# Loads of q and k into alternate partitions, and an evacuation that writes in token order

## The chip, the core and the metric

The kernel runs on one core of a Trainium2 chip. The metric is device time in microseconds (us). Before the change it is 179.21 us, the median of 3 runs (177.88 to 180.92).

The core's engines work in parallel, each through its own instructions in order. PE is the matmul engine (PEld its weight loads), DVE the vector engine, ACT the scalar engine, POOL the GpSimd engine; SP issues nearly all DMAs, through one queue. Matmuls read SBUF and write PSUM. DVE and ACT read PSUM and write SBUF. Copying a PSUM result into SBUF is called an evacuation here.

## The reference

Attention with a causal window of 128 keys and 4 sink keys, then an RWKV channel mix on its output:

```python
# q, k, v: [4, 8, 768, 64] float32; n_sink 4, window 128
scores = scale * np.matmul(q, k.transpose(0, 1, 3, 2))
keep = is_sink | in_window                    # is_sink: key < 4; in_window: 0 <= query - key < 128
a = softmax(np.where(keep, scores, -1e9))
x = np.matmul(a, v)                           # then laid out as [4, 768, 512]
xk = mu_k * x + (1.0 - mu_k) * x_prev         # x_prev: x one token earlier, zeros first
xr = mu_r * x + (1.0 - mu_r) * x_prev
k = np.maximum(xk @ w_k, 0.0)                 # w_k: 512 x 1024
v = k * k @ w_v                               # w_v: 1024 x 512
out = sigmoid(xr @ w_r) * v                   # w_r: 512 x 512
```

## The kernel before

The work is cut into 12 units: 4 batches of 3 tiles with 256 tokens each. A unit u goes through these stages, named by their lines.

- **Loads.** `load` brings q, k and v of a unit into float32 buffers, three of each kind. v comes in two DMAs over 128 partitions in pieces of 256 B (line 396). Of q and k the units that `by_dma` names (k from unit 4 on, q from unit 8 on) come the same way (line 406). The others, k of units 0 to 3 and q of units 0 to 7, come through line 418: two DMAs, w = 0 and 1, one for each half of the heads. A partition takes four tokens in succession, so that each piece is 1 KB; 64 partitions hold the 256 tokens of one half of the heads. Unit 0 is loaded in twice as many DMAs of 128 KB, the others in DMAs of 256 KB. `load_weight` brings the weights in pieces of 2 KB (line 437), 1 MB in a DMA.
- **Prepare.** For each half of what a partition holds: a cast to bf16 (lines 603 and 606, on ACT, DVE or POOL), four PE transposes into one PSUM bank (line 631), and one evacuation into `kt` or `qt` (line 639, on ACT or DVE), which holds the two head pairs with head dimension on partitions and tokens in order along the row. Units that `by_dma` names use a DMA transpose (line 620) in place of the last two. For the first tile of a batch POOL copies the sink keys out of `kt` (line 670).
- **Attend.** Scores on PE (line 716), exponentials on ACT (`e`, line 768), the mask on DVE (line 782), values on PE (line 801), then a reciprocal and a scaling on DVE (lines 815 and 818).
- **Mix and channel mix.** PE transposes `x` (line 841), ACT or DVE evacuates it into `xt` (line 850), DVE makes `xk` and `xr` (lines 868 and 879), PE multiplies by w_k (line 930), ACT takes the relu (line 940), DVE squares it (line 952), PE multiplies by w_r (line 961) and w_v (line 979), DVE combines and SP stores (lines 988 and 995).

The order on every engine is written out by hand: `ORDER` lists operation numbers for PE, DVE, ACT, POOL and SP, and `CHOICE` says which engine does an operation that could run on several. `Plan.schedule` follows these lists and only decides which buffer is used and where filler matmuls go (line 999; they keep PE busy at the start and compute nothing). On SP a DMA that has to wait holds all later ones. What decides when the q and k of a unit can be used is therefore: the place of its two DMAs in SP's list, the queue in front of them, the cast, the transposes, and the evacuation of line 639. The scores of a unit need `kt` and `qt`, and PE's next instructions stand behind those scores.

There are 24 evacuations at line 639: 19 on ACT and 5 on DVE. 28 DMAs come from line 418.

Of the kernel before, what the change touches and what calls it, by code (L numbers as in the profile page):

```python
# [305 lines left out]
def kernel(  # L306
# [55 lines left out]
    buf = P.buf  # L362
# [5 lines left out]
    def dve(n, rate=1.04):  # L368
        return 64.0 + rate * n

    def act(n):
        return 67.0 + 0.833 * n
# [13 lines left out]
    def by_dma(name, u):  # L386
        return u in (KD if name == "k" else QD)

    def load(u, names, rank, h0=0, h1=H):
        b, T = divmod(u, NT)  # L390
        for name in names:
            key = (name, u)
            if name == "v":
                for g in range(2):
                    s0 = 256 * T + 128 * g
                    P.op("SP", 560.0, lambda key=key, g=g, s0=s0: nc.sync.dma_start(
                        out=buf[key][:, g, :, :],
                        in_=v[b, :, s0:s0 + 128, :].rearrange("h p d -> p h d")), rank,
                        service=1330.0, descs=1024, take=[] if g else [("vs", key)],
                        hold=[key] if g else [], writes=[(name, u, g)])  # L400
                continue
            src = {"k": k, "q": q}[name]
            if by_dma(name, u):
                for g in range(2):
                    s0 = 256 * T + 128 * g
                    P.op("SP", 560.0, lambda key=key, src=src, g=g, s0=s0: nc.sync.dma_start(
                        out=buf[key][:, 4 * g:4 * g + 4, :, :].rearrange("p h j d -> p (h j) d"),
                        in_=src[b, :, s0:s0 + 128, :].rearrange("h p d -> p h d")), rank,
                        service=1330.0, descs=1024, take=[] if g else [(name + "s", key)],
                        hold=[key] if g else [], writes=[(name, u, g)])  # L410
                continue

            rows = src[b, :, 256 * T:256 * T + 256, :].rearrange(
                "(w l) (p j) d -> w p l (j d)", w=2, j=4)
            c0, c1 = h0 // 4, h1 // 4
            for w in range(2):
                P.op("SP", 400.0 + 20.0 * (c1 - c0), lambda key=key, rows=rows, w=w: (
                    nc.sync.dma_start(  # L418
                        out=buf[key][64 * w:64 * w + 64, h0:h1].rearrange(
                            "p (l x) j d -> p l (x j d)", x=2),  # L420
                        in_=rows[w][:, 2 * c0:2 * c1])), rank,
                     service=128 * (c1 - c0) * 3.33 + 45.0, descs=128 * (c1 - c0),
                     take=[] if h0 or w else [(name + "s", key)],
                     hold=[key] if h0 or w else [],
                     writes=[(name, u, c, w) for c in range(c0, c1)])
# [14 lines left out]
    for i, what in enumerate(LOADS):  # L440
        if what[0] == "w":
            load_weight(what, i - 100)
        elif what == "kq0":
            load(0, "kq", -100, 0, 4)
            load(0, "kq", -99.5, 4, 8)
        else:
            load(int(what[-1]), what[:-1], i - 100)
# [7 lines left out]
    for i, src in enumerate((moe_mu_k, moe_mu_r)):  # L455
        P.op("ACT", 450.0, lambda i=i, src=src: nc.scalar.dma_start(
            out=rows8[NC * i:NC * i + NC, :], in_=src.rearrange("(c p) -> c p", p=128)), -100,
# [124 lines left out]
    for i in range(4):  # L582
        j = i % 2
# [5 lines left out]
    for i in range(4):  # L589
        j = i % 2  # L590
# [4 lines left out]
    def prepare(u, rank):  # L595
        b, T = divmod(u, NT)
        for name, half in (("k", 0), ("q", 0), ("k", 1), ("q", 1)):
            key, psk = (name + "t", u), ("prep", u, name, half)
            raw, rk = (name, u), (name + "b", u)
            hs = slice(4 * half, 4 * half + 4)  # L600
            def cast(copy, raw=raw, rk=rk, hs=hs, half=half, name=name):
                if by_dma(name, u):
                    return lambda: copy(
                        out=buf[rk][:, half, :, :].rearrange("p h d -> p (h d)"),
                        in_=buf[raw][:, hs, :, :].rearrange("p h j d -> p (h j d)"))
                return lambda: copy(
                    out=buf[rk][:, half, :, :].rearrange("p (j a) d -> p a j d", a=2),
                    in_=buf[raw][:, hs, :, :].rearrange("p (a x) j d -> p a (x j) d", a=2))

            P.op("ACT", act(512), cast(nc.scalar.copy), rank + half,  # L610
                 alts={"ACT": (act(512), cast(nc.scalar.copy), False),
                       "DVE": (dve(512, 0.52), cast(nc.vector.tensor_copy), True),
                       "POOL": (600.0, cast(nc.gpsimd.tensor_copy), True)},
                 take=[] if half else [(name + "b", rk)],
                 hold=[raw] + ([rk] if half else []),
                 reads=[(name, u, half)] if by_dma(name, u) else [(name, u, half, w) for w in range(2)],
                 writes=[rk + (half,)])

            if by_dma(name, u):
                P.op("SP", 1200.0, lambda key=key, rk=rk, half=half: nc.sync.dma_start_transpose(  # L620
                    out=buf[key][:, :, half, :],
                    in_=buf[rk][:, half, :, :].rearrange("p h d -> p (h d)")), rank + half,
                    service=930.0, descs=512, lag=1450.0, room=1200, reads=[rk + (half,)],
                    take=[] if half else [(name + "t", key)],
                    hold=[rk] + ([key] if half else []), writes=[key + (half,)])
                continue

            def transpose(half=half, psk=psk, rk=rk):
                ps = buf[psk].bitcast(BF16)[:, 0:512].rearrange("p (j t) -> p j t", j=4)
                for j in range(4):  # L630
                    nc.tensor.transpose(  # L631
                        out=ps[:, j, :], identity=ident,
                        in_=buf[rk][:, half, 2 * j:2 * j + 2, :].rearrange("p a d -> p (a d)"))

            P.op("PE", 225.0, transpose, rank + half, lag=PE_LAG, take=[("bank", psk)],
                 reads=["ident", rk + (half,)], writes=[psk], hold=[rk])

            def evacuate(copy, half=half, psk=psk, key=key):
                return lambda: copy(  # L639
                    out=buf[key][:, half::2, :, :].rearrange(  # L640
                        "p c g (t j) -> p c j (g t)", j=4),
                    in_=buf[psk].bitcast(BF16)[:, 0:512].rearrange(
                        "p (j c t) -> p c j t", c=2, j=4))

            P.op("ACT", 600.0, evacuate(nc.scalar.copy), rank + half,
                 alts={"ACT": (600.0, evacuate(nc.scalar.copy), False),
                       "DVE": (625.0, evacuate(nc.vector.tensor_copy), False)},
                 hold=[psk] + ([key] if half else []),
                 take=[] if half else [(name + "t", key)],
                 reads=[psk] + ([key + (0,)] if half else []), writes=[key + (half,)])  # L650
# [15 lines left out]
        def sink_keys():  # L666
# [10 lines left out]
            out=buf[psk].rearrange("p (h d) -> p h d", h=H), lhsT=spread,  # L677
# [3 lines left out]
            out=vsink[b % 2][:, :, 0:D], op=ALU.mult, in1=hmask[:, :, 0:D],  # L681
# [370 lines left out]
```

## Time and profile before

| | |
|---|---|
| median of 3 runs | 179.21 us |
| the profiled execution's own time | 178.31 us |
| span of that execution, first to last instruction | 176.6 us |
| PE busy | 161.1 us (91%) |
| DVE busy | 157.1 us (89%) |
| ACT busy | 134.6 us (76%) |
| POOL busy | 19.7 us (11%) |
| bytes by DMA | 33.83 MB, mean 192 GB/s |

The span leaves 1.7 us of the execution's time around it. "Busy" is the time in which an engine had at least one instruction under way. The DMA share of a stretch is the time that all packets took divided by the time of 16 DMA engines; it can go over 1 where packets of one engine overlap. Times of a row start at the beginning of the span.

### The profile page before, as it was taken

The page shows a single profiled execution, that of the slowest core. Times are in us where ns is not written, and L with a number is a line of the kernel's source. Part 1 is how long each engine was busy: PE and PEld are TensorE (multiplying, and loading weights), DVE is VectorE, ACT ScalarE, POOL GpSimd, SP SyncE. Part 2 cuts the span into 40 slices and gives each one's busy share as a digit, 9 for nine tenths or more (in the row PEclk, how much of TensorE's full clock was granted, in tenths as well). Part 3 has the DMA queues.
Part 4 walks back from the last instruction along what each step waited for, and adds up shares of the span by engine and source line. Part 5 has one row for each costly group of instructions (what it writes and reads, how often), then busy time and mean ns, then how long its engine had stood idle before and what let it go on. Part 6 is the DMA issues. An engine that isn't in the chain of part 4 may idle for free.

```text
span 176.6 us, 4238 instructions
## 1 busy us (share of the span) xinstructions
PE 161.1 (91%) x1603; PEld 102.9 (58%) x1603; DVE 157.1 (89%) x399; ACT 134.6 (76%) x200; POOL 19.7 (11%) x45
## 2 busy tenths in 40 slices
PE   7875668889979999999999999999999999999992
PEld 2334445655545756765655777575466576677551
DVE  5579998999979998999999999998999799997851
ACT  2383899999799999799889999666768949845020
POOL 7513001020212200333100000000000100000000
PEclk9998799999999999999999999999999999999999
DMA  3799999979999999989989789587888953130043
GB/s 91 208 236 236 387 224 315 317 248 240 213 229 198 231 166 231 241 173 186 205 197 261 138 170 272 111 197 185 210 203 205 226 116 114 39 142 0 2 178 119
DMA packets 75844, 33.83 MB, mean 192 GB/s; under 512 B 63912, under 2 KB 70320, under 8 KB 75824
## 3 DMA queue, kind: packets, MB, share of 16 engines
q1 hardware_dynamic: 75808, 33.56, 82.4%
q8 instruction: 12, 0.20, 0.5%
q14 instruction: 8, 0.07, 0.2%
q10 hardware_dynamic: 16, 0.00, 0.0%
HBM read 24.12 MB, written 6.29 MB: 172 GB/s over the span
## 4 chain that ended last, share of the span: by engine, by line
PE 55%; ACT 16%; DMA 8%; DVE 8%; SPq 6%; issue 3%; POOL 0%; DVEq 0%; ACTq 0%; POOLq 0%
PE bank L930 16%; PE bank L979 16%; PE bank L961 8%; SPq L418 6%; DMA qs<-in_q_dram 5%; ACT qt L639 5%; PE bank L801 5%; ACT e L768 5%; PE sc L716 4%; DMA ks<-in_k_dram 3%; DVE xr L879 2%; PE bank L841 2%; ACT kt L639 2%; PE bank L756 2%; ACT xt L850 1%
## 5 line engine op out<-in xcount | busy, mean ns | idle before, releaser
L930 PE MATMUL bank<-xk,wk_sb 128*128 128x256 bf16 x384 | 51.0, 273 | 2.6 <-ACT wk_sb L568 1.7
L768 ACT ACTIVATE e<-sc 128x1024 bf16<-128x1024 f32 (+1 forms) x48 | 45.5, 978 | 3.4 <-PE sc L716 3.4
L979 PE MATMUL bank<-wv_h,kk 128*128 128x512 bf16 x184 | 46.4, 379 | 0.1
L930 PEld LDWEIGHTS <-wk_sb 128*128 128x128 bf16 x384 | 35.5, 98 | 13.1 <-issue 2.3
L940 ACT ACTIVATE rl<-bank 128x512 bf16<-128x512 f32 x44 | 26.4, 619 | 8.3 <-PE bank L930 5.1
L782 DVE TENSOR_TENSOR e<-e,mask 128x1024 bf16<-128x1024 bf16 (+1 forms) x48 | 30.2, 641 | 0.4 <-ACT e L768 0.4
L979 PEld LDWEIGHTS <-kk 128*128 128x128 bf16 x184 | 16.8, 98 | 14.9 <-issue 0.6
L961 PE MATMUL bank<-wr_sb,xr 128*128 128x512 bf16 x96 | 24.2, 379 | 0.1
L879 DVE SCALAR_TENSOR_TENSOR xr<-td,mu_all,xt 128x256 bf16<-128x256 bf16 x48 | 22.9, 492 | 0.1
L967 ACT ACTIVATE th<-bank 128x512 f32<-128x512 f32 x24 | 14.5, 618 | 10.3 <-PE bank L961 10.3
L879 DVE SCALAR_TENSOR_TENSOR xk<-td,mu_all,xt 128x256 bf16<-128x256 bf16 x48 | 21.9, 487 | 0.1
L952 DVE TENSOR_TENSOR kk<-rl 128x512 bf16<-128x512 bf16 x48 | 19.9, 429 | 0.5 <-ACT rl L940 0.4
L818 DVE TENSOR_TENSOR x<-bank,rec 128x256 bf16<-128x256 f32 x48 | 19.4, 418 | 0.5
L639 ACT COPY qt<-bank 128x512 bf16<-128x512 bf16 x13 | 17.3, 1333 | 2.9 <-PE bank L631 2.9
L988 DVE SCALAR_TENSOR_TENSOR ob<-th,bank 128x512 f32<-128x512 f32 x23 | 15.7, 683 | 3.7 <-PE bank L979 2.9
L801 PE MATMUL bank<-vb,e 128*128 128x65 bf16 x352 | 16.2, 193 | 2.0 <-DVE e L782 2.0
L801 PEld LDWEIGHTS <-e 128*128 128x128 bf16 x352 | 13.8, 97 | 5.3 <-DVE e L782 2.3
L716 PE MATMUL sc<-qt,kt 64*128 64x128 bf16 (+1 forms) x256 | 14.5, 242 | 2.6 <-ACT qt L639 1.1
L716 PEld LDWEIGHTS <-kt 64*128 64x128 bf16 x256 | 9.8, 96 | 7.9 <-issue 4.4
L961 PEld LDWEIGHTS <-xr 128*128 128x128 bf16 x96 | 9.0, 98 | 8.7 <-issue 0.6
L850 ACT COPY xt<-bank 128x512 bf16<-128x512 bf16 x16 | 9.5, 594 | 2.3 <-PE bank L841 2.2
L868 DVE TENSOR_TENSOR td<-xt 128x512 bf16<-128x512 bf16 x24 | 10.2, 434 | 0.8 <-ACT xt L850 0.8
(71 smaller groups left out, 160.3 us busy)
## 6 DMA issues: line engine op xcount, KB each, us to landing
vs<-in_v_dram SPq DMA_DIRECT2D x24, 256.0 KB, 5.1
out_dram<-ob SPq DMA_DIRECT2D x23, 256.0 KB, 2.9
qs<-in_q_dram SPq DMA_DIRECT2D x22, 256.0 KB, 4.8
ks<-in_k_dram SPq DMA_DIRECT2D x22, 256.0 KB, 5.5
w<-in_moe_w_k_dram SPq DMA_DIRECT2D x2, 1024.0 KB, 12.2
w<-in_moe_w_v_dram SPq DMA_DIRECT2D x2, 1024.0 KB, 9.3
w<-in_moe_w_r_dram SPq DMA_DIRECT2D x1, 1024.0 KB
ks<-in_k_dram SPq DMA_DIRECT2D x4, 128.0 KB, 2.9
```

The source lines that it names most:

```text
L639: return lambda: copy(out=buf[key][:, half::2, :, :].rearrange("p c g (t j) -> p c j (g t)", j=4), in_=buf[psk].bitcast(BF16)[:, 0:512].re ...
L716: nc.tensor.matmul(out=sc[:, a, o0:o1], lhsT=lhs[rows], rhs=rhs[rows], start=u not in BIAS, stop=True, skip_group_check=u in BIAS)
L768: nc.scalar.activation(out=buf[ek][:, :, lo:], in_=buf[sck][:, :, lo:], func=AF.Exp, scale=scale)
L782: nc.vector.tensor_tensor(out=at, in0=at, in1=m, op=ALU.mult)
L801: nc.tensor.matmul(out=o[:, g, a, :], lhsT=e[:, a, e0:e0 + 128], rhs=rhs, start=(T == 0 and i == 0), stop=(i == len(blocks) - 1), skip_gro ...
L818: P.op("DVE", dve(256), lambda ok=ok, rk=rk, c=c: nc.vector.tensor_tensor(out=buf["x", u][:, :, 128 * c:128 * c + 128].rearrange("p g (a d ...
L879: nc.vector.scalar_tensor_tensor(out=buf[key][:, c0 + 2 * i, :], in0=buf[tk][:, i, :], scalar=mu[w][:, c0 + 2 * i:c0 + 2 * i + 1], in1=xt[ ...
L930: nc.tensor.matmul(out=ps[:, i, :], lhsT=wk_sb[:, c, 128 * f:128 * f + 128], rhs=xk[:, c, :], start=(c == 0), stop=(c == NC - 1), skip_gro ...
L940: nc.scalar.activation(out=buf[rk], in_=buf[psk].rearrange("p (i t) -> p i t", i=2), func=AF.Relu)
L952: P.op("DVE", dve(512, 0.52), lambda f2=f2, rk=rk: nc.vector.tensor_tensor(out=buf["kk", u][:, 2 * f2:2 * f2 + 2, :], in0=buf[rk], in1=buf ...
L961: nc.tensor.matmul(out=buf[psk], lhsT=buf["xr", u][:, c, 128 * g:128 * g + 128], rhs=wr_sb[:, c, :], start=(c == 0), stop=(c == NC - 1))
L979: nc.tensor.matmul(out=buf[psk], rhs=wv_h[:, f, :], lhsT=buf["kk", u][:, f, 128 * g:128 * g + 128], start=(f == 0), stop=(f == NF - 1))
```

## The change

The destination of the two loads of line 418 changes from partitions 0 to 63 (w = 0) and 64 to 127 (w = 1) to the even (w = 0) and the odd (w = 1) partitions. Source, size of the pieces and number of DMAs stay.

A transposed partition is a column of the PSUM bank, so the columns of the two halves of the heads now alternate. The evacuation's access patterns change with that. Before, it reads runs of 64 adjacent bf16 columns and writes each run at a step of four elements (8 bytes). After, it writes runs of 256 adjacent elements and reads, for each group of four, one element from each of the four transposes: a step of 128 elements (256 bytes) inside the group, and of two elements (4 bytes) from group to group.

```diff
@@ load, line 418
-                        out=buf[key][64 * w:64 * w + 64, h0:h1].rearrange(
+                        out=buf[key][w::2, h0:h1].rearrange(
                             "p (l x) j d -> p l (x j d)", x=2),
                         in_=rows[w][:, 2 * c0:2 * c1])), rank,
@@ prepare, line 639
             def evacuate(copy, half=half, psk=psk, key=key):
                 return lambda: copy(
                     out=buf[key][:, half::2, :, :].rearrange(
-                        "p c g (t j) -> p c j (g t)", j=4),
+                        "p c g (t j) -> p c (g t) j", j=4),
                     in_=buf[psk].bitcast(BF16)[:, 0:512].rearrange(
-                        "p (j c t) -> p c j t", c=2, j=4))
+                        "p (j t c) -> p c t j", c=2, j=4))
```

The instructions on every engine, their order, their number and what they wait for are the same in both kernels; only the access patterns of these two operations differ.

## Prediction

> **What bounds the kernel now.** I read the chain of waits first, then a table of engine times by stage, the groups by form, and ACT's order of time in the stage where it is full. The chain, pieces in order of time (start, length, what):
>
> ```profile
> 9.73 5.72 DMA ks<-in_k_dram
> ...
> 16.89 1.31 DVE kt L639
> 18.24 0.62 PE sc L716 x6
> ...
> 20.71 1.31 ACT kt L639
> ...
> 39.09 8.96 DMA qs<-in_q_dram
> ...
> 48.65 1.30 ACT qt L639
> ```
>
> Until 57 us the end is set by three things in turn: loads of q and k (5.72 and 8.96 us of waiting), evacuations of line 639, and ACT's other work. From 57 to 83 the chain alternates between ACT and DVE; from 83 on it holds only PE, so what is saved earlier is kept and nothing more is won there. The stages, with their busy times, granted clock, DMA share and rate:
>
> ```profile
> core 0: us, PE busy (x) PEld busy (x) DVE busy (x) ACT busy (x) POOL busy (x), PEclk, DMA share, GB/s
> 0.00:20.00 20.00, 15.04 (x120) 7.95 (x121) 14.71 (x43) 9.84 (x11) 7.59 (x27) 0.91 0.86 216
> 20.00:36.00 16.00, 11.43 (x148) 8.57 (x146) 14.82 (x36) 15.98 (x21) 0.61 (x1) 1.00 1.02 288
> 36.00:48.00 12.00, 11.32 (x108) 6.24 (x106) 11.71 (x29) 10.82 (x16) 1.75 (x2) 1.00 1.04 244
> 48.00:57.00 9.00, 7.74 (x72) 4.41 (x71) 7.76 (x16) 8.66 (x12) 2.12 (x4) 1.00 1.12 213
> 57.00:83.00 26.00, 25.59 (x270) 17.48 (x268) 25.12 (x64) 24.79 (x38) 6.07 (x7) 1.00 1.13 206
> ```
>
> ACT is full from 20 to 36 us (15.98 of 16). DVE stands right behind it: 14.82 there, and 11.71 of 12 in the next stage. So freeing ACT is worth only what DVE has idle, and what the loads allow.
>
> **The evacuations.** Groups by form (busy, mean ns of one):
>
> ```profile
> L639 ACT COPY qt<-bank 128x512 bf16<-128x512 bf16 x13 | 17.3, 1333 | 2.9 <-PE bank L631 2.9
> ...
> L815 DVE RECIPROCAL rec<-bank 128x4 f32<-128x4 f32 x48 | 7.8, 176 | 3.1 <-PE bank L801 2.5
> ...
> L850 ACT COPY xt<-bank 128x512 bf16<-128x512 bf16 x16 | 9.5, 594 | 2.3 <-PE bank L841 2.2
> ...
> L639 DVE COPY qt<-bank 128x512 bf16<-128x512 bf16 x3 | 3.9, 1294 | 0.5 <-PE bank L631 0.5
> ...
> L944 DVE TENSOR_SCALAR rl<-bank 128x512 bf16<-128x512 f32 x4 | 2.7, 686 | 0.4 <-PE bank L930 0.4
> ```
>
> Line 639 moves as many elements as line 850, which reads and writes without a step, yet takes 1333 ns against 594. Its read is already in runs of 64, so I put the 0.7 us down to the write at 8-byte steps; that ACT and DVE take nearly the same (1333, 1294), though their stepless rows differ, fits a cost that lies in the memory. The change removes that step and adds another, a read of PSUM at 256 bytes. No row shows such a read at size. Bounds: at best it costs nothing, 594 ns on ACT and 415 on DVE, as line 850 has there. The nearest row with any step is line 639 itself, 1.31 us: no change. The far end is line 815, which reads four values 260 bytes apart in 176 ns, while a copy of eight adjacent ones (line 557) takes 134: if the whole difference were the step, 10 ns an element, 5 us an evacuation; the reciprocal itself explains it better. Nothing excludes a loss. I take 0.65 us on ACT and, from line 944, 0.69 on DVE, since every row that writes in runs lies there and the far end rests on one row with another explanation.
>
> How much of ACT's time an evacuation holds is seen in its order of time:
>
> ```profile
> 20.71 1.31 ACT L639 COPY kt<-bank 128x512 bf16<-128x512 bf16 x1
> 21.73 1.13 ACT L568 ACTIVATE wk_sb<-w 128x1024 bf16<-128x1024 f32 x1
> ...
> 24.77 0.63 ACT L940 ACTIVATE rl<-bank 128x512 bf16<-128x512 f32 x1
> 25.24 0.43 ACT L700 ACTIVATE es<-bank 128x256 bf16<-128x256 f32 x1
> ```
>
> The next instruction starts 1.02 us after an evacuation, and 0.47 us after a stepless 512-element one. So each evacuation frees about 0.5 us of ACT and shortens the wait of whoever needs it by 0.65.
>
> [...]
>
> **The loads.** Rates by stretch:
>
> ```profile
> 4.00:6.00 2.00, 2.00 (x7) 0.54 (x6) 0.66 (x2) 0.00 (x0) 1.87 (x7) 1.00 0.65 212
> 12.00:14.00 2.00, 0.90 (x14) 0.54 (x14) 1.46 (x6) 1.51 (x2) 0.00 (x0) 1.00 1.13 229
> ...
> 18.00:20.00 2.00, 1.89 (x25) 1.45 (x25) 2.00 (x7) 1.61 (x3) 0.00 (x0) 0.63 1.05 386
> ```
>
> While loads of line 418 queue (12 to 14 us) they move 229 GB/s with all 16 DMA engines held, 1.13 x 16 / 229 = 79 ns for each KB; spaced by SP's issue (4 to 6 us) a KB takes 0.65 x 16 / 212 = 49 ns; weights, over 128 partitions, go at 386 GB/s. So queued loads into 64 adjacent partitions slow each other. The change spreads each over the whole height. Bounds: 229 (no change) and 386; below 229 I have no row, and nothing excludes it. I take the middle, 300: 256 KB take 0.87 us in place of 1.14, 0.27 less for each DMA. The piece size, the number and SP's issue time (0.6 us each) stay, so I cost the issue at nothing.
> [...]
>
> **The sum, stage by stage**, where the advance is the smallest that any needed engine allows:
> - 0 to 20: k of unit 1 lands after four queued DMAs, 4 x 0.27 = 1.1 us earlier, but DVE is full from 14 to 16, so its `kt` evacuation at 16.89 moves only by idle time (0.2) and by what the earlier evacuations give (0.4, held by v's arrival), and is 0.6 shorter: 1.2 us.
> - 20 to 36: ACT frees 5 x 0.5 = 2.5 us. DVE has 1.2 idle and 0.4 from its one evacuation, 1.6 in all. I take 1.1: 2.3 in all.
> - 36 to 48: PE waits at 45.25 for k of unit 3, and the load of q ends the 8.96 us wait. By then 8 + 3 queued DMAs have gained 11 x 0.27 = 3.0 us, more than 2.3, so the loads don't eat the advance. PE and DVE are full: 0.
> - 48 to 57: four evacuations on ACT and one on DVE; PE is idle 1.26, DVE 1.24. I take 1.0: 3.3.
> - 57 to 83: four on ACT (two on the chain, at 63.86 and 68.11), but DVE has 0.9 idle and PE 0.4: 0.5, so 3.8.
> - after 83: two on ACT, beside a full PE: 0.
>
> 178.31 - 3.8 = 174.5 us for an execution like the profiled one, which lies 0.90 under the median of the runs: 175.4 us as a median. The cast, transposes and sink copy read the same amounts and cost nothing more; the clock of 0.63 at 18 to 20 us may move by some tenths either way.
>
> **The rivals.** (2) The loads reach the weights' rate: 256 KB in 0.68 us, 0.46 less; 45.25 then never binds and the first stage gives a little more. DVE still limits: 4.6 in all, 174.6. (3) The loads stay at 229: then k of unit 3 lands at 44.5 as before and PE's 2.3 us are lost waiting for it; left are 0.7 (the shorter `qt` at 48.65), 1.0 and 0.5: 2.2, so 177.0. For it: each DMA still has only 64 rows. (4) The stepped read costs what the stepped write did: ACT stays full, loads alone give 0.9, 178.3. (5) Slower: the read costs more than the write did. ACT has no slack from 20 to 36 and 0.3 from 48 to 57, so every 0.1 us above 1.31 costs 0.1 for each of 5 + 4 + 2 evacuations; at 1.65 us it is 2% slower, at double the present 1.02 us of ACT's time it is +11, less 0.9 from the loads: 189. Against it: rows that write in runs. (6) The stepped destination slows the loads, or their issue: if each of the 0.6 us issues of unit 0 doubled, the start would move by 8 x 0.6 less what the fast evacuations give: 182.
>
> **How the numbers follow.** Forecast 0.40 (own range 174.2 to 176.8), rivals 0.18, 0.20, 0.09, 0.09 and 0.04. About 2% (3.6 us) is what a measurement of this kernel can tell from no change. Under 175.6 lie 0.25 of the forecast's 0.40, 0.16 of (2) and 0.03 of (3): faster 0.44. Over 182.8 lies (5) and most of (6), 0.13 with a rest: slower 0.13; within, 0.43. The range 172.2 to 180.0 takes in the first four cases with their errors and leaves out (5), (6) and some 0.06 below.
>
> **What would show it.** Right: line 639 near 650 ns on ACT and 690 on DVE; 12 to 14 us, or wherever q and k queue, near 300 GB/s; k of unit 3 before 42.5 us; ACT no longer full from 20 to 36; PE reaching its unbroken stretch about 3.8 us sooner. Wrong: line 639 at 1.3 us or more; 229 GB/s again, with PE waiting before 45 us; or DVE with idle time where I said that it limits.

## The result and the profile after

| | before | after |
|---|---|---|
| median | 179.07 us of 4 runs (177.88 to 180.92) | 171.11 us of 4 runs (170.57 to 172.68) |
| ratio | | 0.9591, 95% interval 0.9499 to 0.9682 |
| the profiled execution, its span | 178.31 us, 176.6 us | 170.57 us, 168.9 us |
| PE, DVE, ACT busy | 161.1, 157.1, 134.6 us | 157.9, 153.4, 123.4 us |

The medians differ by 8.0 us; the ratio leaves out one execution of before that was in a slower state (180.92 us), and by it the gain is 7.3 us. The forecast was a gain of 3.8 in the profile, where 7.7 came, and 171.11 lies under the whole range. In a second comparison the same kernel had 0.9612 (0.9524 to 0.97).

The stages of the changed kernel, columns as in the table of before:

```profile
core 0: us, PE busy (x) PEld busy (x) DVE busy (x) ACT busy (x) POOL busy (x), PEclk, DMA share, GB/s
0.00:20.00 20.00, 15.22 (x130) 8.20 (x132) 14.57 (x46) 9.01 (x12) 7.74 (x27) 0.91 0.83 260
20.00:36.00 16.00, 13.79 (x172) 10.17 (x173) 15.84 (x38) 15.71 (x25) 1.22 (x2) 1.00 0.96 276
36.00:48.00 12.00, 11.90 (x115) 6.65 (x113) 11.97 (x32) 9.82 (x17) 1.80 (x4) 1.00 1.07 282
48.00:57.00 9.00, 9.00 (x103) 6.41 (x102) 8.96 (x26) 8.44 (x15) 2.57 (x3) 1.00 1.00 219
57.00:83.00 26.00, 25.59 (x287) 17.09 (x286) 25.79 (x66) 23.47 (x40) 5.24 (x6) 1.00 0.97 216
```

DVE has 0.44 us of idle time in the 63 us from 20 to 83, where it had 3.59. ACT, full before from 20 to 36 us, is still near full there (15.71), but it does more in that time: the stage now holds 25 of its instructions, not 21.

The groups of the copies (busy, mean ns of one):

```profile
L850 ACT COPY xt<-bank 128x512 bf16<-128x512 bf16 x16 | 9.5, 591 | 2.9 <-PE bank L841 2.9
...
L639 ACT COPY qt<-bank 128x512 bf16<-128x512 bf16 x13 | 7.7, 594 | 4.6 <-PE bank L631 4.6
...
L639 DVE COPY qt<-bank 128x512 bf16<-128x512 bf16 x3 | 2.1, 687 | 0.9 <-PE bank L631 0.9
```

On ACT the evacuation that reads at 256-byte steps takes 594 ns, the same as line 850 (591), which reads without a step. On DVE it takes 687.

ACT's order of time after one of them:

```profile
21.04 0.57 ACT L639 COPY qt<-bank 128x512 bf16<-128x512 bf16 x1
21.50 1.03 ACT L768 ACTIVATE e<-sc 128x1024 bf16<-128x1024 f32 x1
```

It holds ACT for 0.46 us, where it held it for 1.02.

The rates of two stretches, the first of them with loads of line 418 queued as in the same stretch of before:

```profile
12.00:14.00 2.00, 0.08 (x3) 0.08 (x4) 2.00 (x7) 0.30 (x1) 0.00 (x0) 1.00 1.05 335
40.00:42.00 2.00, 1.91 (x22) 1.03 (x21) 2.00 (x5) 1.44 (x4) 0.63 (x1) 1.00 1.14 344
```

The last number is the rate: 229 GB/s became 335. The second stretch of before, where loads of line 418 are queued too:

```profile
40.00:42.00 2.00, 2.00 (x20) 1.04 (x17) 1.85 (x7) 2.00 (x4) 0.00 (x0) 1.00 1.08 236
```

236 GB/s became 344.

The chain of waits, pieces in order of time:

```profile
5.50 0.60 SPq L418
6.15 0.60 SPq L396
6.80 3.91 DMA vs<-in_v_dram
...
18.77 0.69 DVE qt L639
...
21.64 1.81 DVE e L782 x3
...
29.73 1.19 DVE xk L879 x3
...
40.91 0.61 DVE ob L988
41.95 0.48 PE bank L801 x16
42.43 1.73 PE bank L979 x8
...
59.10 0.43 DVE xk L879 x2
...
75.67 0.61 DVE vsink L680
```

The waits for q and k are gone from it, and so are ACT's evacuations. From 18.77 to 41.5 us almost every piece is work of DVE; then they are PE's up to 59 us, DVE's again from 59.10 to 76.3, and PE's from there on.

### The profile page after: what moved, and what is told of

Same layout as the page of the kernel before. It is cut to its first block, busy times and chain, and to the rows that moved or that the text cites. A ratio compares the mean times of both kernels' runs of the same rounds, so it can differ in the third digit from the quotient of the medians.

```text
span 168.9 us, 4238 instructions
## 1 busy us (share of the span) xinstructions
PE 157.9 (94%) x1603; PEld 102.1 (60%) x1603; DVE 153.4 (91%) x399; ACT 123.4 (73%) x200; POOL 19.6 (12%) x45
## 4 chain that ended last, share of the span: by engine, by line
PE 66%; DVE 24%; SPq 3%; DMA 2%; issue 2%; DVEq 0%
PE bank L979 20%; PE bank L930 17%; PE bank L961 9%; DVE e L782 6%; PE bank L801 5%; PE sc L716 5%; DVE xr L879 4%; SPq L418 3%; PE bank L841 3%; DVE xk L879 3%; PE bank L631 3%; DMA vs<-in_v_dram 2%; DVE x L818 2%; DVE kk L952 2%; PE bank L756 1%
## 5 line engine op out<-in xcount | busy, mean ns | idle before, releaser
L768 ACT ACTIVATE e<-sc 128x1024 bf16<-128x1024 f32 (+1 forms) x48 | 44.9, 961 | 5.5 <-PE sc L716 5.5
L940 ACT ACTIVATE rl<-bank 128x512 bf16<-128x512 f32 x44 | 25.8, 605 | 9.4 <-PE bank L930 5.7
L639 ACT COPY qt<-bank 128x512 bf16<-128x512 bf16 x13 | 7.7, 594 | 4.6 <-PE bank L631 4.6
```

The lines of the kernel that those rows point to most:

```text
L768: nc.scalar.activation(out=buf[ek][:, :, lo:], in_=buf[sck][:, :, lo:], func=AF.Exp, scale=scale)
L940: nc.scalar.activation(out=buf[rk], in_=buf[psk].rearrange("p (i t) -> p i t", i=2), func=AF.Relu)
```

## The experiments

The theory to be tested, A: neither edit can bring its gain alone, because the slow loads hold what the evacuations free and the full ACT holds what the loads free; with both, DVE's time is what remains. The comparisons with the kernel before were made again in each group of runs (179.05, 178.69, 178.46 and 177.91 us), so ratios to it are what is compared.

**Evacuations alone.** Both writes of line 418 go to halves again; line 639 keeps the write in runs and reads to suit.

```diff
-                        out=buf[key][w::2, h0:h1].rearrange(
+                        out=buf[key][64 * w:64 * w + 64, h0:h1].rearrange(
...
-                        "p (j t c) -> p c t j", c=2, j=4))
+                        "p (j c t) -> p c t j", c=2, j=4))
```

> The loads go to halves again; the evacuation reads the four transposes in turn (256-byte step, 2 bytes from group to group) and writes adjacent elements. Same output. Line 639 near 594 ns on ACT and 692 on DVE in all theories. Theory A (both parts are needed: with loads at 229 GB/s, k of unit 3 lands near 44.5 us as before and PE's advance of about 3 us before it is lost in waiting): the gain is what lies behind 45 us, 4 to 5 us, so about 174.5 us, with queued loads at 229 GB/s and PE idle before the transposes of unit 3. Theory B (the evacuations carry it all, the loads were hidden): 171 to 172 us.

176.83 us (176.11 to 177.65), ratio 0.9879 (0.9813 to 0.9944): a gain of 2.2 us. The stage from 36 to 48 us, and two pieces of the chain:

```profile
36.00:48.00 12.00, 9.40 (x96) 5.41 (x95) 9.70 (x24) 8.08 (x14) 1.35 (x2) 1.00 0.96 231
```

```profile
38.02 13.53 DMA ks<-in_k_dram x2
51.55 0.40 DVE xk L879
```

PE, DVE and ACT all have idle time here, 2.6, 2.3 and 3.9 us of 12, and the chain holds 13.53 us of waiting for loads of k. The shorter evacuations are paid out as waiting. Theory A's signs were there, 229 GB/s from 12 to 14 us and 1.3 us of PE's waiting for k of unit 3, but its number, about 174.5, was 2.3 us too low: the loads hold more of the gain than it thought. (The profiled execution is the longest of the four, 177.65 us.)

**Loads alone.** Alternate partitions, but the evacuation writes in steps of 8 bytes as before.

```diff
-                        "p c g (t j) -> p c (g t) j", j=4),
+                        "p c g (t j) -> p c j (g t)", j=4),
...
-                        "p (j t c) -> p c t j", c=2, j=4))
+                        "p (j t c) -> p c j t", c=2, j=4))
```

> The loads go to alternate partitions; the evacuation still writes at 8-byte steps (it reads every second column of a transpose). Same output. Line 639 near 1.3 us in all theories. Theory A (ACT stays full from 20 to 36 us, so earlier loads have nothing to speed): 177.5 to 178.5 us, queued loads at 335 GB/s or more. Theory C (the loads were the main cost, the evacuations lay beside them): 174 us or less.

177.49 us (177.29 to 177.97), ratio 0.9926 (0.9894 to 0.9958): a gain of 1.3 us by the ratio. The stage from 20 to 36 us:

```profile
20.00:36.00 16.00, 11.71 (x144) 8.67 (x144) 14.85 (x36) 15.98 (x22) 1.89 (x2) 1.00 0.95 276
```

ACT is full to 0.02 us again. The loads moved 321 GB/s from 12 to 14 us (335 or more was expected), and POOL cast its half of k of unit 3 3.3 us earlier than in the kernel before, to no use: ACT cast the other half only 0.7 us earlier (43.82 for 44.53 us). By the ratios the two edits alone gain 1.2 and 0.7%, together 4.1% (3.9 in the second comparison): about 2%, 3.5 us, exists only when both are made.

**Stepped writes on one engine.** The changed kernel, but the evacuations of one engine write in steps again: DVE's five, then ACT's nineteen.

```diff
             def evacuate(copy, half=half, psk=psk, key=key):
+                stepped = copy == nc.vector.tensor_copy      # nc.scalar.copy in the second
                 return lambda: copy(
                     out=buf[key][:, half::2, :, :].rearrange(
+                        "p c g (t j) -> p c j (g t)" if stepped else
                         "p c g (t j) -> p c (g t) j", j=4),
                     in_=buf[psk].bitcast(BF16)[:, 0:512].rearrange(
+                        "p (j t c) -> p c j t" if stepped else
                         "p (j t c) -> p c t j", c=2, j=4))
```

> The changed kernel, but the 5 evacuations on DVE write at 8-byte steps; the 19 on ACT don't. Same output. Theory A' (DVE is what limits until 83 us once ACT is free, so all of its time counts one for one): 5 x 0.48 us come back, 173.0 to 173.8 us. Rival D (DVE has slack, what counts is the waits for a single evacuation): 171 to 172 us.

> The changed kernel, but the 19 evacuations on ACT write at 8-byte steps; the 5 on DVE don't. Same output. Theory A' (ACT is full from 20 to 36 us again and sets the pace there, in front of DVE): 175 to 177 us. Rival E (DVE's 3 us are what counts, ACT has slack enough): 171.5 to 172.5 us.

DVE's: 173.55 us (171.91 to 174.62), ratio 0.9678 (0.9597 to 0.9759). By the ratios 1.6 us are lost for 5 x 0.61 us of work, about half, and the interval overlaps that of the changed kernel: the direction is as expected, the size isn't settled by this run. ACT's: 177.27 us (176.82 to 178.41), ratio 0.9936 (0.99 to 0.9971): 6.2 us are lost, more than expected, and ACT is full from 20 to 36 us once more (15.99 of 16). So ACT's evacuations carry most of the gain, on the condition that the loads keep up.

**Which loads matter.** All evacuations write in runs; alternate partitions only for units 0 to 2, only from unit 3 on, or only for unit 3.

```diff
-                        out=buf[key][w::2, h0:h1].rearrange(
+                        out=buf[key][slice(w, 128, 2) if u < 3 else slice(64 * w, 64 * w + 64), h0:h1].rearrange(
...
-                        "p (j t c) -> p c t j", c=2, j=4))
+                        "p (j t c) -> p c t j" if u < 3 else "p (j c t) -> p c t j", c=2, j=4))
```

(u >= 3 and u == 3 in the other two.)

> The changed kernel, but only the loads of units 0 to 2 go to alternate partitions; k of unit 3 and q of units 3 to 7 go to halves again, and their evacuations read accordingly (still writing in token order, 0.59/0.69 us each). Evacuations alone gave 176.8, both edits 171.1. Theory A (evacuations alone lose their gain at two places: behind the slow queue of 10 to 16 us, and at 45 us behind k of unit 3, and the second is only late because its issue and its rate did not move): the advance at 28 us is the changed kernel's (2.5 to 3 us), k of unit 3 is issued near 33 us and cast near 42, about 1.2 us later than in the changed kernel, and the time is 172 to 174. Rival B (each fast load brings its own share, 6 of the 12 k and q tensors early and 6 late): about 174, and the advance at 28 us is half the changed kernel's, near 2. Rival C (all that matters is k of unit 3): 176 to 177, and PE stands at 44 us as with evacuations alone.

> The other half: only k of unit 3 and q of units 3 to 7 go to alternate partitions, units 0 to 2 to halves; all evacuations write in token order. Theory A: the queue of 10 to 16 us is slow again (229 GB/s), the advance at 28 us is about 1.0 as with evacuations alone, k of unit 3 is no longer late, so the 1.2 us lost at 44 us come back: 174.5 to 176. Rival B: about 174. Rival C: 171 to 173. If e5 and this one give the changed kernel's gain together (5.7 us beyond evacuations alone), the loads' part adds up; if the sum is smaller, they need each other too.

> The changed kernel, but only the loads of unit 3 (k and q, four transfers of 256 KB) go to alternate partitions; all others go to halves, and all evacuations write in token order. Evacuations alone gave 176.8; with unit 3 and all later units on alternate partitions it was 172.5. In those runs the second issue of k of unit 3 stood 7.5 to 7.6 us before k's last cast with halves and 6.1 us with alternate partitions, and the first issue of the unit 12.5 us before q's last cast with halves, 10.0 with alternate partitions. Theory D (what holds the evacuations' gain is the queue of 35 to 46 us, in which k and q of unit 3 wait): k cast about 1.4 us and q about 2.5 us earlier against their issues again, PE without a gap over 1 us between 40 and 48 us, and 172.3 to 173.7. Rival E (the later units' q, which share the queue with v and k of later units, matter as much): 174 to 175.5, with PE's gaps coming after 48 us.

Units 0 to 2: 174.89 us, ratio 0.9804 (0.975 to 0.9857). From unit 3 on: 172.48, ratio 0.9687 (0.9626 to 0.9748). Unit 3 alone: 174.76 (173.85 to 176.44), ratio 0.98 (0.9699 to 0.9901), which its interval doesn't part from evacuations alone. In parts of the time before, the first two gain 0.0075 and 0.0192 over evacuations alone, 0.0267 together; both edits everywhere gain 0.0288 or, in the second comparison, 0.0267. The loads' part adds up within the intervals, and 0.7 of it comes from unit 3 on. The times of unit 3, read from SP's issues, POOL's cast of half of k, and the landing of q:

| kernel | second issue of k to POOL's cast | second issue of q to its landing |
|---|---|---|
| before | 37.09 to 44.58: 7.49 us | 8.5 us |
| evacuations alone | 38.02 to 45.66: 7.64 | 8.4 |
| units 0 to 2 alternate | 35.74 to 43.29: 7.55 | 8.4 |
| unit 3 alternate | 37.21 to 44.66: 7.45 | 8.5 |
| loads alone | 35.16 to 41.26: 6.10 | 6.1 |
| unit 3 on alternate | 36.60 to 42.74: 6.14 | 5.9 |
| after | 34.63 to 40.76: 6.13 | 6.2 |

With alternate partitions k comes 1.4 us and q 2.4 us sooner after its issue; the early loads bring the issue itself forward. (The 12.5 and 10.0 us for q in the last expectation end at POOL's cast of q of unit 4, not 3, and unit 4 goes to halves in that run; the 8.96 us wait in the chain of before is for q of unit 4, too.) Theory A's sizes for the two halves fell (it put more on the early loads), and so did rival B's equal shares; rival C missed the time of the early ones and had that of the late ones, but not its reason, as unit 3 alone shows. Its own transfers are on alternate partitions there, yet the second k and the second q land as late as with halves. The stretches of that run, and two of the run with alternate partitions from unit 3 on:

```profile
40.00:42.00 2.00, 1.95 (x17) 1.06 (x14) 1.97 (x6) 1.74 (x3) 0.00 (x0) 1.00 1.03 345
42.00:44.00 2.00, 2.00 (x14) 0.71 (x11) 2.00 (x5) 1.45 (x3) 0.00 (x0) 1.00 1.12 213
44.00:46.00 2.00, 0.62 (x19) 0.61 (x18) 0.86 (x3) 0.79 (x2) 0.68 (x1) 1.00 1.16 188
```

```profile
42.00:44.00 2.00, 2.00 (x24) 1.00 (x22) 2.00 (x5) 1.44 (x4) 0.61 (x1) 1.00 1.12 339
44.00:46.00 2.00, 2.00 (x22) 1.06 (x19) 2.00 (x8) 1.60 (x3) 0.61 (x1) 1.00 1.34 235
```

With unit 3 alone 345 GB/s at first, then 213 and 188, under the 226 to 239 of the kernel before at that time; with unit 3 on, 339 and 235. SP issues k, q and k of unit 3, then q of unit 4, q of unit 3 and q of unit 4. Up to the first q of unit 4 these two kernels are the same, and until k and q of unit 3 have landed they differ only in the destination of q of unit 4. From issue to landing the first k took 5.9 us in both, the second k 6.0 us with unit 3 on and 7.3 with unit 3 alone, the second q 5.9 and 8.5. So q of unit 4 in halves slows the transfers of unit 3 that are in flight with it, those issued ahead of it too; each kernel was profiled once. Theory D fell on that. Rival E had the time, though PE's gap came before 48 us (0.62 us of work in the third line), not after.

**What a step costs.** Twenty copies of 128x512 appended to the changed kernel, on constant data; here the bf16 writes from PSUM and the others that decide.

```diff
         P.run()
+        nc.scalar.copy(out=sb[:, 0:512], in_=ps[:, 0:512])          # line 1023, write step 1
+        nc.scalar.copy(out=sb[:, 0:1024:2], in_=ps[:, 0:512])       # 1024, step 2
+        nc.scalar.copy(out=sb[:, 0:2048:4], in_=ps[:, 0:512])       # 1025, step 4
+        nc.scalar.copy(out=sb[:, 0:4096:8], in_=ps[:, 0:512])       # 1026, step 8
...
+        nc.scalar.copy(out=sf[:, 0:1024:2], in_=ps[:, 0:512])       # 1028, f32, step 2
...
+        nc.vector.tensor_copy(out=sb[:, 0:512], in_=ps[:, 0:512])   # 1037
...
+        nc.vector.tensor_copy(out=sb[:, 0:512], in_=ps[:, 0:1024:2])  # 1043, read step 2
...
+        nc.vector.tensor_copy(out=sb[:, 0:2048:4], in_=so[:, 0:512])  # 1046, SBUF to SBUF, step 4
```

> The changed kernel with 20 copies of 128x512 appended after its end, on constant data: on ACT, then on DVE, from a PSUM bank as bf16 to SBUF with steps of 1, 2, 4 and 8 elements in the write, to f32 with steps of 1 and 2, a read in steps of 2 from PSUM, and SBUF to SBUF plain, with the read in steps of 4 and with the write in steps of 4. The dear 1.31 us of the kernel before had writes at a step of 4 elements (8 bytes) and the cheap 0.59 us reads at a step of 128. Theory A (the cost is of a bf16 write whose step is not 1, per element, 2 to 2.6 ns): all stepped bf16 writes take near 1.3 us on both engines, plain ones 0.59 (ACT) and 0.69 or less (DVE), stepped reads as plain ones, and f32 writes near 0.6 to 0.7 for both steps. Rival B (the cost grows with the step): the write at step 2 lies between, near 0.9, that at step 8 above 1.31, near 2.5. Rival C (a cost of the pair PSUM to SBUF): SBUF to SBUF with the write in steps of 4 stays under 0.8.

Groups by form (busy, mean ns of one):

```profile
L1040 DVE COPY w<-bank 128x512 bf16<-128x512 bf16 x1 | 2.4, 2430 | 0.0
L1026 ACT COPY w<-bank 128x512 bf16<-128x512 bf16 x1 | 2.4, 2424 | 0.0
...
L1025 ACT COPY w<-bank 128x512 bf16<-128x512 bf16 x1 | 1.3, 1292 | 0.0
...
L1046 DVE COPY w<-w 128x512 bf16<-128x512 bf16 x1 | 0.7, 735 | 0.0
L1024 ACT COPY w<-bank 128x512 bf16<-128x512 bf16 x1 | 0.7, 727 | 0.0
...
L1043 DVE COPY w<-bank 128x512 bf16<-128x512 bf16 x1 | 0.7, 691 | 0.0
...
L1028 ACT CAST w<-bank 128x512 f32<-128x512 bf16 x1 | 0.6, 615 | 0.0
...
L1023 ACT COPY w<-bank 128x512 bf16<-128x512 bf16 x1 | 0.6, 585 | 5.8 <-DVE w L1018 5.8
...
L1037 DVE COPY w<-bank 128x512 bf16<-128x512 bf16 x1 | 0.4, 359 | 0.0
```

Rival B holds: the cost of a bf16 write grows with its step, 585, 727, 1292 and 2424 ns on ACT for 1, 2, 4 and 8 elements. An f32 write by ACT at 8-byte steps costs next to nothing (615 ns, 585 without a step), where bf16 at the same 8 bytes doubles the copy (1292 against 585). A read at a step of 2 elements is free on ACT (585 ns, line 1029), but on DVE it costs 691 against 359. Rival C holds in part: DVE from SBUF to SBUF takes 735 with the step of 4 in the write, though without a step it takes 293; ACT takes 1326, and 618 without a step.

**Three attempts at a better version.** The changed kernel with q of unit 0 issued by ACT's queue:

```diff
-            for w in range(2):
-                P.op("SP", 400.0 + 20.0 * (c1 - c0), lambda key=key, rows=rows, w=w: (
-                    nc.sync.dma_start(
+            own = ("ACT", nc.scalar) if key == ("q", 0) else ("SP", nc.sync)
+            for w in range(2):
+                P.op(own[0], 400.0 + 20.0 * (c1 - c0), lambda key=key, rows=rows, w=w, own=own: (
+                    own[1].dma_start(
```

> The changed kernel, with the four loads of q of unit 0 issued by ACT's queue ahead of everything else, so that SP issues k of unit 0 and then v of unit 0: SP's issues take 0.65 us each and the chain begins with eight of them before v (6.15 us). Theory A (the changed kernel's start is held by the issues): v is issued near 3.5 us, the first casts begin about 1 us sooner, and the chain that DVE carries from 18 us begins 1 to 2 us sooner: 169.2 to 170.3. Rival B (the start is held by the transfers, or by what DVE has to do before 18 us): k and q land no earlier since they share the queues' engines, 171 +- 0.6. Rival C (ACT's issues delay its table load and the first evacuation): 171.5 to 173.

with four of DVE's operations given to ACT (and moved in the two lists):

```diff
-    "POOL", 144: "DVE", 145: "DVE", 148: "POOL", 151: "DVE", 153: "DVE", 154: "DVE",
-    155: "DVE", 157: "DVE", 164: "DVE", 196: "POOL", 205: "DVE", 209: "ACT", 230:
+    "POOL", 144: "ACT", 145: "ACT", 148: "POOL", 151: "ACT", 153: "DVE", 154: "DVE",
+    155: "DVE", 157: "DVE", 164: "DVE", 196: "POOL", 205: "ACT", 209: "ACT", 230:
```

> The changed kernel with four of DVE's operations of 12 to 17 us (the two casts of q of unit 1, 0.42 us each, the evacuation of k of unit 1, 0.69, and a cast of q of unit 2, 0.42) given to ACT, which is idle for 3.7 us there. Theory F (from 18 to 41 us the end hangs on DVE's unbroken work, so what DVE is spared before that brings everything forward, since DVE's stepped evacuations alone had cost 2.4 us for 5 x 0.61): 1.0 to 1.9 us less than the changed kernel of the same call. Rival G (before 18 us DVE waits for PE or for the loads, and what it is spared turns into idle time): within 0.5 us of it, with DVE idle 1 us or more longer in 12 to 20 us.

and with fillers in PE's gap (operation 134 is the first after it):

```diff
+            if i == 134:
+                b = min(free["bank"])
+                order += [("fill", self.pools["bank"][b[1]])] * 7
             if o["engine"] == "PE" and self.fill:
```

> The changed kernel with seven more filler matmuls of line 999 (0.25 us each) in PE's gap of 2.0 us that begins near 11.9 us. In the changed kernel's two profiles the granted clock is 0.5 from 14.6 to 18 us in one and from 13.8 to 20.2 us in the other, and PE stands 0.9 us further back at 36 us in the second; the times spread from 170.6 to 173.2. Theory H (the gap brings the half clock on): no stretch at 0.5 before 21 us, PE about 0.5 to 1 us further ahead at 36 us than in the first of them, 169.3 to 170.6 with less spread. Rival I (the half clock comes whatever PE does in the gap): it stays, 171.1 to 172.1. Rival J (more work brings more of it, or the fillers delay what follows them): the half clock lasts longer, 172.2 or more.

> The changed kernel as it is, on the chip of this call, as the measure for the two others: 171.1 +- 0.8.

172.44 us, ratio 0.9677 (0.9632 to 0.9722); 171.52, ratio 0.9638 (0.9551 to 0.9726), beside 0.9612 (172.12 us) of the changed kernel in the same group; 172.34, ratio 0.9674 (0.9571 to 0.9778). None can be told from the changed kernel. In the first, v was issued at 3.83 us, but the first cast began at 5.58, where it was 4.69, and ACT's first evacuation at 6.89, where it was 5.72: rival C, with the late k and q of rival B. In the second, DVE was busy 5.64 of the 8 us from 12 to 20, where it had 7.62 and 6.57 in the two profiles of the changed kernel: rival G, the time spared turned into idle time. In the third the half clock was gone (the granted clock is the third number from the end):

```profile
12.00:14.00 2.00, 1.67 (x7) 0.58 (x6) 2.00 (x7) 0.36 (x1) 0.00 (x0) 1.00 1.09 332
14.00:16.00 2.00, 1.73 (x27) 1.40 (x28) 2.00 (x7) 0.85 (x2) 1.50 (x4) 1.00 0.98 350
16.00:18.00 2.00, 2.00 (x33) 1.44 (x31) 2.00 (x7) 1.46 (x3) 0.00 (x0) 1.00 1.05 388
```

The waits of its next stage, 20 to 36 us (total, times, longest):

```profile
ACT vb L656 <- DMA vs<-in_v_dram: 1.5, 1, 1.5
...
DVE wv_h L575 <- DMA w<-in_moe_w_v_dram: 1.3, 1, 1.3
```

Theory H was right of the clock, in the one execution profiled, and wrong of the time, which was rival J's: DVE now waits 1.3 us for a weight and ACT 1.5 us for v. The DMA share is 0.98 to 1.09 in the three stretches above, at 332 to 388 GB/s: the DMA engines had packets under way nearly all of that time. That they hold the start was not shown.

## Why the prediction was wrong

What held, by its own steps:

- The evacuations: 0.65 and 0.69 us were taken, 0.594 and 0.687 measured. The lower bound was right on ACT. The fear of the stepped read was unfounded on ACT (594 ns beside the 591 of line 850; 585 ns with a step of 2 and without one in the probe); on DVE there is such a cost, 0.33 us in the probe (691 ns against 359), and the value from line 944 covered it, though for another reason. The write was the dear side, as was assumed: 1292 ns at a step of 4 in bf16 on ACT, 585 without a step.
- ACT's hold of an evacuation: about 0.5 us less was taken, 0.56 measured.
- The loads: 300 GB/s was taken, 335 and 344 measured in the two stretches. Why a load into 64 alternate partitions is faster than one into 64 adjacent ones, no run here shows.
- k of unit 3 before 42.5 us: 40.76.
- One sign did not come: ACT, forecast to be no longer full from 20 to 36 us, was busy 15.71 of 16, with more instructions in that time.
- Rival 3, loads at 229: 177.0, and evacuations alone gave 176.83, for the reason given there (k of unit 3 came even later, at 45.66). Rival 4, loads' gain alone: 0.9, measured 1.3.

What failed is the sum stage by stage. The advance of the same PE instruction from the trace of before to that of after, matched by line and order:

| by | forecast | measured |
|---|---|---|
| 20 us | 1.2 | 1.4 |
| 36 us | 2.3 | 3.1 |
| 48 us | 2.3 | 3.9 |
| 57 us | 3.3 | 5.8 |
| 83 us | 3.8 | 7.1 |
| the end | 3.8 | 7.7 |

The step said that the advance is the smallest that any needed engine allows, and named DVE as that engine; then it took less than DVE allows: 1.1 of 1.6 us from 20 to 36, nothing of 0.3 from 36 to 48, 1.0 of 1.24 from 48 to 57, without the 0.6 of DVE's own evacuation there, and 0.5 of 0.9 after that, where PE's 0.4 idle was held against it. DVE between the same two instructions, from the evacuation at 20.20 us to line 988 at 83.03 of before, and after:

```profile
20.20:83.03 62.83, 55.89 (x586) 36.49 (x584) 59.29 (x142) 60.09 (x86) 10.55 (x14) 1.00 1.08 235
```

```profile
18.77:76.20 57.43, 54.16 (x586) 36.28 (x584) 57.09 (x142) 52.93 (x87) 10.21 (x14) 1.00 0.99 252
```

The same 142 instructions of DVE (third busy time) take 57.43 us, 57.09 of them busy. 5.40 us are gained: 3.20 from idle time (3.54 to 0.34) and 2.20 from work, of which the two evacuations in this stretch are 1.22. The rest, about 1.0, is other work of DVE that got shorter, chiefly lines 879 and 653 (0.45 and 0.42 us); why was not tried. The forecast for these stages was 2.6. Taken whole, DVE's idle time in the four stages (3.59 us) and its two evacuations (1.22) make 4.8; with the 1.2 before 20 us that would have put the profiled execution at 172.3 us, and it took 170.57. The other 1.7 us are chiefly the shorter other work of DVE (about 1.0) and what came after 83 us (0.7), both of which the sum put at nothing. That DVE holds the whole stretch is read from this balance and the chain; the run that gave DVE its stepped evacuations back lost only about half of the added work, so it supports this in direction, not in size.

One reading of the chain was wrong as well: from 57 to 83 us it does not alternate between ACT and DVE, but is PE's up to 60.85, ACT's to 69.95 and DVE's from there on, so from 70 us on DVE was what an edit had to relieve.

Two reasons why PE didn't hold it, as the step assumed with "PE and DVE are full". PE's busy time in this stretch fell too, 55.89 to 54.16, for the same 586 matmuls: a busy PE was not a PE at its peak. And the 36 to 48 us in which nothing was to be won were held by the loads, which the table of unit 3 shows to have moved by 1.4 us for k and 2.4 for q, beside their earlier issue; evacuations alone leave 2.6 us of PE idle there.

Since the forecast and the second rival stopped at the same DVE allowances, that rival, with loads faster than they were, gave only 4.6, and the range had no case that could reach 171. After 83 us the forecast was nothing; 0.7 us came, most of it between 120 and 144 us, and where from stays open.

## What to carry to other kernels

Where one engine is named as the limit, balance it over the whole stretch between two of its instructions, its idle time and the work taken off it, and take that as the gain unless another wait is shown to come last (here 3.5 and 1.2 us, of 5.4 measured); shares taken "to be safe" stage by stage add up to a wrong size. Two edits that remove waits of the same buffers must be summed together, not each on its own: here 1.2 and 0.7% alone made 4.1% together. Put the step of a bf16 evacuation of PSUM on the side of the read (here 594 ns in place of 1333 on ACT, 687 in place of 1294 on DVE), and spread loads that don't fill the partitions over the whole height (here 335 GB/s in alternate partitions from 12 to 14 us, in place of 229 in adjacent ones).

## What the runs showed of the hardware

- The cost of a bf16 write by ACT from PSUM grew with its step, 585, 727, 1292, 2424 ns for 512 elements at 2, 4, 8 and 16 bytes; an f32 write at 8 bytes took 615 (one execution).
- DVE copied 512 bf16 from PSUM in 359 ns without a step and in 691 ns with a read at a step of 2 elements; ACT took 585 for both (the same execution).
- Transfers to adjacent halves slowed transfers to alternate partitions that were in flight with them, also those issued ahead: 7.3 us from issue to landing in place of 6.0 for the second k of unit 3, 8.5 in place of 5.9 for the second q, in one execution of each kernel.
- A gap of 2.0 us on PE near 12 us was followed by a granted clock of 0.5, for 3.4 us in one execution of the changed kernel and for about 6.8 us in another; with fillers in the gap, in one execution, the clock stayed at 1.00.
